# Mish's products in quarters and normalising products in halves, shared between VectorE and GpSimd

## The chip, the cores and the metric

The kernel runs on one core of one Trainium2 chip. The metric is the device time of one execution in microseconds (us), from a few runs of the same program; lower is better.

## What is computed

The reference mixes two branches over the same input x (2048 tokens of 640 values) with one gate per token:

```python
x = A_x
g = _sigmoid((x * gate_w).sum(-1, keepdims=True))
a = _A_ref(x, A_wqkv, A_wo)     # softmax attention, 32 heads of 20, then @ wo
b = _B_ref(x, B_w1, B_b1, B_w2) # h = x@w1 + b1;  h * tanh(softplus(h));  @ w2
return g * a + (1 - g) * b
```

The activation h·tanh(log(1+exp h)) is Mish, over 2048 x 1536 values. Attention has 32 heads x 2048 x 2048 scores, and every one of them goes through an exponential.

## The kernel before

**Units and slots.** The scores are cut into 2048 units of 128 keys x 512 queries. A *group* (c, g) is one chunk c of 512 queries with four heads g; it has 64 units. The program goes through them in 683 slots of three units (`NSLOT`). For each slot TensorE writes three blocks of 512 columns into PSUM (`score_mms`, L1330), and ScalarE takes the exponential of them in one ACTIVATE (`emit_e`, L1351). TensorE multiplies the results with V into one PSUM bank for the group (`pv`, L1669).

**Units given to VectorE.** In many slots the third unit is not given to ScalarE. VectorE evicts it from PSUM as a 16-bit integer that serves as a rough exponential (`emit_x`, L1400). Two more VectorE passes from SBUF to SBUF, over up to four such units at a time, make two shifted copies (`shift`, L1438), and TensorE multiplies all three with V. ScalarE then has an ACTIVATE of 1024 columns in that slot instead of 1536. `choose` (L1497) decides for each slot whether a unit is given away: it adds up how far VectorE is behind and what is waiting for it, and refuses from `BEHIND`, from `crowded` (`IDLE`, `IDLE_2`: how much may wait when the slots before gave one too), when tasks are late (`CATCH_UP`, `LAG`), or when `room` finds that the rest would not fit. `NUDGE` is a list of 87 hand-set values, one for every eight slots, which shifts that sum.

**Other work.** Everything else is put in between: projections of q, k and v, the Mish branch (`h_task`: x@w1 and a bias add on VectorE, L1040; then `mish`; then `b_task`: @w2), and the output products (`p_task`, `part_task`). One Mish covers 128 x 1024 values and there are 24 of them. Each is a tanh on ScalarE (L1063) and then a chain of eight VectorE steps, each of which reads what the one before wrote: a 16-bit copy W, three short tensor-scalar steps (both L1087), and four products of two 16-bit tensors (L1090). W and the second tensor B exist once, so one Mish is in work at a time. The steps wait in the queue `blend`, which is worked off from its head.

**Normalising.** When a group is finished, its sums are copied out of PSUM (L1849). Its 128 x 16 denominators go by DMA to another layout, are inverted on GpSimd with a power instruction (`invert`, L1871), and go by DMA through DRAM to all rows (L1874, L1880). Then one product of 128 x 512 normalises the group (`times`, L1805). For the last groups of the last chunk (`DIRECT`) VectorE makes the inverse by itself with two transposes (L1860 to L1862). The partial output products of the last chunk (`part_task`) are placed by `PART_DUE`.

**What sets the order.** The whole order is worked out in Python when the program is built. `Plan` keeps a clock for each engine; `Plan.add` appends an instruction, advances the clock by a cost constant (`WIDE` 0.60 us for a wide VectorE pass, `EXP` 1.335 and `EXP_PAIR` 0.908 for the two kinds of ACTIVATE, `INVERT`, `ASIDE` for GpSimd) and records semaphore waits. The times of the plan are not the chip's: on the chip only the order on each engine and the waits hold. `work` fills VectorE with waiting jobs before an eviction is due. After each eviction `settle` (L498) looks back at VectorE's line in the plan: instructions from SBUF to SBUF carry the mark "L". If the head of `blend` or `norm` may go to GpSimd, if it is ready, and if its GpSimd cost and 0.1 us fit between the last such instruction and VectorE's clock, it is put on GpSimd, with a wait for that last instruction. Before, this holds for the normalising product alone, as a whole. `patient` keeps a job from VectorE until a short time after it is ready. `load` counts a job that may go to GpSimd with 0.3 (`SHARE`) of its cost.

Of the kernel before, what the change touches and what calls it, by code (L numbers as in the profile page):

```python
# [14 lines left out]
ALU = mybir.AluOpType  # L15
# [14 lines left out]
CW = 512  # L30
# [4 lines left out]
SCALE = DH ** -0.5  # L35
EW = DH + 1
NETS = 6
OLD = 3
WAITED = 2
OWE = 0.1  # L40
SLOT = 3
HALF = D // 2

# [20 lines left out]
FLEX = 1  # L64
TOP_UP = 0
SX = 285
SX_STEP = 15
AWAIT = 0.01
SHARE = 0.3
AWAIT_1 = 0  # L70
# [4 lines left out]
LANES = 2  # L75
TAKEN = 3.6
LATE_OFF = 0.4
SLACK = 0.2
LATER = 0.5
FREE = 0  # L80
# [9 lines left out]
NEAR = 0.2  # L90
STORED = 1.0
TALL = 0.1
BEYOND = 0.4
SOONER = 9
KT_AHEAD = 5
NEXT_KT = 2
QUAD = 0.60
# [13 lines left out]
EAGER = 90  # L111
LOAD = 0.95
MISH = 4
GROUP = 3.0
LAST = 0
END = 55
SHIFT = 0.5
LAG = 50
SPARE = 3
WINDOW = 4.0  # L120
CALM = 2
PACKED = 5
PACKED_Q = 21
Q_AT = 120
Q_STEP = 21
SQ = 40
SQ_STEP = 16
H_AT = 150
H_STEP = 14
# [25 lines left out]
WARM = 7  # L155
FETCH = (2.3, 3.0)
LEAD = 16
NUDGE = [0.8, -6, -3.5, -3.7, 3.7, 3, -3.7, 3, -3, 1.5, 1.5, 5.3, 3.7, 3, -0.7, -1.5, 6, 0.0, 6, 0.7, -0.7, -5.2, 0.7, -0.7, 0, 3.7, -3, 1.5, 0.7, -4.3, 2.2, 5.3, 3.7, 1.5, 1, 2.2, -0.8, 2.1, 2.9, 2.3, 1.5, 6, 5.0, 5.9, -3, -2.3, -2.3, 1.5, 1.5, 1.5, 1.5, 2.0, 1.5, -5, -3.5, 0.8, 5, 0.0, 0.7, 2.9, 0.7, 1.5, 0, 6, 6, 5, 3.6, 6, 6, 5.8, 6, -0.8, 3.8, 1.5, 2.2, 5.7, 0.7, 5, 6, 2.2, 6, 4.5, 3.0, -1.5, 5, 0.5, 5]


class Op:
# [113 lines left out]
def bass_gated_mix__softmax_full_mha__dense_activation_mish__prompt_kernel(  # L275
# [44 lines left out]
    RR = sb("RR", [P, 16], FP32)  # L320
# [36 lines left out]
    BC = BCT[:, :]  # L357
# [72 lines left out]
    def attention(pl, fast):  # L430
# [3 lines left out]
        at = {}  # L434
# [63 lines left out]
        def settle():  # L498

            while fast:  # L500
                for todo in (blend, norm):
                    job = todo[0][5] if todo and len(todo[0]) > 5 else None
                    ready = job and job[0]()
                    if not ready:
                        continue
                    line = pl.line
                    i = len(line)
                    while i and not line[i - 1][2]:
                        i -= 1
                    begin = max(ready.t1 + HOP, pl.now["pool"], line[i - 1][0])  # L510
                    while i < len(line) and line[i][0] <= begin:
                        i += 1
                    if begin + job[1] + APART <= pl.now["dve"]:
                        todo.popleft()
                        job[2](line[i - 1][1])
                        break
                else:
                    return

        def patient(op, wait):  # L520

            return now["step"] < NSLOT - CALM_END and pl.now["dve"] < op.t1 + wait
# [86 lines left out]
        if fast:  # L609
# [448 lines left out]
            def mish(ev, hb, hc, k):  # L1058


                h = hb.rearrange("p i t -> p (i t)")
                U = AREAS[6 * hc + k >= FIRST][2]
                ex = pl.add("act", lambda e: e.activation(U, h, AF.Tanh, scale=0.5, bias=-MISH_AT), [ev, u_free[0]], cost=0.95)  # L1063
                u_free[0] = "busy"
                last = [ex]
                due = ex.t1 + PATIENCE

                def piece(cost, fn, after=None, wait=0):
                    def run(eng="dve", *more):
# [12 lines left out]

                W, B = (U2[:, n * CW:(n + 1) * CW].bitcast(FP16) for n in range(2))

                def scalar(dst, src, one, two=None):
                    ops = (one, two, ALU.mult, ALU.add) if two is not None else (one, None, ALU.add)
                    return lambda e: e.tensor_scalar(dst, src, *ops)  # L1087

                def times(dst, one, two):
                    return lambda e: e.tensor_tensor(dst, one, two, ALU.mult)  # L1090
# [5 lines left out]
                piece(WIDE, times(B, B, B))  # L1096
                piece(QUICK, scalar(B, B, MISH_BY, MISH_BY * MISH_OUT), None, AWAIT_1)
                piece(WIDE, times(B, W, B))
                piece(WIDE, times(h, B, h), done)

            def b_task(hc, t, half, due):
                c, part = divmod(hc, 2)
# [663 lines left out]
        def group_done(c, g, step, last):  # L1766
# [36 lines left out]
            def times(src, deps, eng="dve"):  # L1803
                to = otn(c, g, fast) if direct else OTN[:, moves[0] % 2, NFT, :]
                op = oung_free[0] = bc_read[0] = otn_done[(c, g)] = pl.add(eng, lambda e: e.tensor_tensor(  # L1805
                    to, src, BC, ALU.mult), [*deps, *reads()], cost=WIDE if eng == "dve" else ASIDE, kind="L")
# [63 lines left out]
            def invert():  # L1870
# [1 line left out]
                    RR[:, :], RR[:, :], NEG[:, :].to_broadcast([P, 16]), ALU.pow), [got, m_neg], cost=INVERT)  # L1872
                     if fast else pl.add("dve", lambda e: e.reciprocal(RR[:, :], RR[:, :]), [got], cost=0.25))
                rr_read[0] = pl.add("sp", lambda e: e.dma_start(  # L1874
                    SUMS.ap().rearrange("j (r a) -> (j r) a", a=16), RR[:, :]), [r, *spread_last], "nr1", cost=0.4, tail=2.8)
                norm.append((0.0, spread, lambda: rr_read[0]))

            def spread():
                for j in range(HG):
# [4 lines left out]
                norm.append((WIDE, lambda: times(src, wide), lambda: False if fast and patient(wide[-1], AWAIT) else wide[-1],  # L1884
                             0, None, (lambda: wide[-1], ASIDE, lambda dep: times(src, [*wide, dep], "pool"))))
            norm.append((0.25, invert, lambda: got))


# [461 lines left out]
```

## Time and profile before

| | |
|---|---|
| median of 3 runs | 761.59 us (760.7 to 762.83) |
| profiled execution: its own time | 759.97 us |
| its span, first to last instruction | 758.2 us |
| granted TensorE clock | 0.997 |
| instructions | 19479 |

The busy times of the engines in the span overlap; a share near 100% means that the engine hardly pauses. An instruction's duration in the trace reaches into the next one's start, so that on a queue without pauses the distance from start to start is what an instruction costs. "Idle before" is time in which the engine waited ahead of an instruction, with what ended the wait behind the arrow. VectorE is DVE in the profile, ScalarE ACT, TensorE PE, GpSimd POOL.

### The profile page before, as it was taken

Reading aid. Unit: us, or ns where it says so; the run is one execution under the profiler, and the core shown is the slowest. Engines: PE = TensorE matmul, PEld = TensorE weight load, DVE = VectorE, ACT = ScalarE, POOL = GpSimd, SP = SyncE. Lnnn points to the kernel's source line nnn. Section 1 sums busy time; section 2 is a strip of 40 time slices with the busy share of each in tenths; the row PEclk is TensorE's granted clock in tenths of the full one; section 3 lists DMA queues with packets and bytes.
Section 4 is the critical chain, followed back from the end, with each engine's and each line's share of the span. In section 5 each row is a group of like instructions: output and inputs, shape, how many; then the busy total and the mean of one; then the engine's idle time right before and its main releaser. Section 6 shows DMA issues by size and latency. Waiting matters only on the chain.

```text
span 758.2 us, 19479 instructions
## 1 busy us (share of the span) xinstructions
PE 717.1 (95%) x8095; PEld 266.2 (35%) x8095; DVE 705.2 (93%) x1275; ACT 742.7 (98%) x714; POOL 124.8 (16%) x62
## 2 busy tenths in 40 slices
PE   8999999999999999999999999999999998999996
PEld 4433332333323333333333344333333333333233
DVE  4789899999999899998989999999999999999997
ACT  6999999999999999999999999999999999999996
POOL 8112120211110121110222100211022110211000
PEclk9999999999999999999999999999999999999999
DMA  8311321211233223150212414021221221010001
GB/s 186 106 56 53 99 64 51 69 54 54 65 94 114 64 65 91 37 147 20 66 43 82 111 32 124 28 70 51 68 62 48 68 67 38 19 31 21 22 8 39
DMA packets 80737, 49.05 MB, mean 65 GB/s; under 512 B 24794, under 2 KB 76882, under 8 KB 80642
## 3 DMA queue, kind: packets, MB, share of 16 engines
q1 hardware_dynamic: 79874, 47.61, 22.4%
q8 instruction: 67, 1.10, 0.6%
q14 instruction: 28, 0.23, 0.1%
q10 hardware_dynamic: 656, 0.10, 0.1%
q0 software_dynamic: 112, 0.01, 0.1%
HBM read 35.57 MB, written 7.51 MB: 57 GB/s over the span
## 4 chain that ended last, share of the span: by engine, by line
ACT 77%; PE 11%; DVE 10%; DMA 1%; issue 0%; SPq 0%
ACT ETS L1351 75%; PE PS L1330 3%; PE PS L1669 3%; PE PS L567 2%; DVE OTN L1400 2%; ACT REG L1063 2%; DVE OTN L1438 1%; PE PS L2077 1%; DVE U L1087 1%; DVE U L1090 1%; DVE REG L1400 1%; DVE HB L1040 1%; ACT W2R L1063 1%; DMA OTN<-in_A_x_dram 1%; DVE QT L1400 1%; DVE PADS L1400 1%
## 5 line engine op out<-in xcount | busy, mean ns | idle before, releaser
L1351 ACT ACTIVATE ETS<-PS 128x1024 bf16<-128x1024 f32 (+1 forms) x683 | 722.4, 1264 | 3.9 <-PE PS L1330 3.3
L1330 PE MATMUL PS<-QT,KT 32*128 32x512 bf16 (+1 forms) x2112 | 270.2, 378 | 22.5 <-ACT ETS L1351 16.4
L1871 POOL TENSOR_TENSOR RR<-RR,NEG 128x16 f32<-128x16 f32 x29 | 90.1, 3106 | 470.4 <-DMA RR<-OUNG 413.8
L1669 PE MATMUL PS<-ETS,V_all 128*21 128x512 bf16 (+1 forms) x1621 | 161.1, 376 | 0.0
L1330 PEld LDWEIGHTS PS<-QT,KT 32*128 32x128 bf16 x2112 | 67.3, 91 | 230.9 <-ACT ETS L1351 182.3
L567 PE MATMUL PS<-XB,REG 128*32 128x256 bf16 (+3 forms) x770 | 82.4, 295 | 4.3 <-DVE HB L1040 2.2
L1400 DVE TENSOR_SCALAR QT<-PS 128x512 int16<-128x512 f32 x116 | 78.4, 684 | 4.8 <-PE PS L1330 3.9
L567 PE MATMUL PS<-W2R,HB 128*32 128x320 bf16 (+1 forms) x747 | 70.3, 300 | 3.3 <-DVE XB L1112 1.5
L1400 DVE TENSOR_SCALAR OTN<-PS 128x512 int16<-128x512 f32 x105 | 70.7, 683 | 1.5 <-PE PS L1330 1.2
L1400 DVE TENSOR_SCALAR PADS<-PS 128x512 int16<-128x512 f32 x85 | 57.1, 682 | 5.5 <-PE PS L1330 5.1
L567 PEld LDWEIGHTS PS<-XB,REG 128*128 128x128 bf16 (+1 forms) x770 | 38.4, 96 | 38.5 <-issue 27.3
L1669 PEld LDWEIGHTS PS<-ETS,V_all 128*21 128x21 bf16 x1621 | 39.2, 90 | 34.4 <-issue 29.8
L1090 DVE TENSOR_TENSOR U<-U 128x1024 f16<-128x1024 f16 x72 | 49.1, 682 | 0.2
L567 PEld LDWEIGHTS PS<-W2R,HB 128*32 128x32 bf16 (+1 forms) x747 | 33.6, 97 | 33.7 <-issue 13.7
L1400 DVE TENSOR_SCALAR REG<-PS 128x512 int16<-128x512 f32 x60 | 40.6, 683 | 2.5 <-PE PS L1330 2.0
L1400 DVE TENSOR_SCALAR KT<-PS 128x512 int16<-128x512 f32 x49 | 33.4, 685 | 3.8 <-PE PS L1330 3.5
L1040 DVE TENSOR_TENSOR HB<-PS,B1T 128x512 bf16<-128x512 f32 x48 | 32.7, 682 | 2.2 <-PE PS L567 2.0
L1805 POOL TENSOR_TENSOR OTN<-OUNG,BCT 128x512 bf16<-128x512 f32 x12 | 15.2, 1270 | 94.8 <-issue 76.7
L1087 DVE TENSOR_SCALAR U<-U 128x1024 f16<-128x1024 f16 x72 | 30.1, 418 | 0.6
L567 PE MATMUL PS<-XB,WOQ 128*128 128x512 bf16 (+1 forms) x146 | 28.6, 382 | 0.7 <-DVE HB L1040 0.5
L1438 DVE TENSOR_SCALAR QT<-QT 128x2048 int16<-128x2048 int16 (+2 forms) x48 | 28.7, 603 | 0.4 <-PE PS L1669 0.4
L1400 DVE TENSOR_SCALAR W2R<-PS 128x512 int16<-128x512 f32 x38 | 25.7, 684 | 2.2 <-PE PS L1330 1.5
(174 smaller groups left out, 778.6 us busy)
## 6 DMA issues: line engine op xcount, KB each, us to landing
REG<-in_B_w_dram SPq DMA_DIRECT2D x36, 320.0 KB, 3.2
BCT<-SUMS SPq DMA_DIRECT2D x116, 64.0 KB, 2.1
W2R<-in_B_w_dram SPq DMA_DIRECT2D x12, 320.0 KB, 3.3
KT<-KS SPq DMA_DIRECT2D x28, 128.0 KB
QT<-QS SPq DMA_DIRECT2D x112, 20.0 KB
QS<-WOQ SPq DMA_DIRECT2D x16, 128.0 KB, 1.8
KS<-OTN SPq DMA_DIRECT2D x16, 128.0 KB, 1.8
W2R<-in_B_w_dram SPq DMA_DIRECT2D x1, 1920.0 KB, 8.4
```

What stands on the lines that cost most here:

```text
L567: op = e.matmul(PS[at, bank, cols], w[:, at], x, start=start, stop=stop, **({"tile_position": (0, i * rows)} if parts > 1 else {}))
L1040: ev = dve(lambda e: e.tensor_tensor(hb, PS[:, bank, :].rearrange("p (i t) -> p i t", i=2), bias, ALU.add), [last, b_load, *b_read.get(hc ...
L1063: ex = pl.add("act", lambda e: e.activation(U, h, AF.Tanh, scale=0.5, bias=-MISH_AT), [ev, u_free[0]], cost=0.95)
L1087: return lambda e: e.tensor_scalar(dst, src, *ops)
L1090: return lambda e: e.tensor_tensor(dst, one, two, ALU.mult)
L1330: op = pl.add("pe", lambda e, i=i, g=real(g), tile=tile, j=j, cols=cols, c=c, of_q=of_q: e.matmul(scores(s)[:, i, cols], KT[32 * j:32 * j ...
L1351: e_op[s] = pl.add("act", lambda e: e.activation(EXPS[:, at:at + n, :], scores(s)[:, 0:n, :], AF.Exp, scale=SCALE, bias=LIFT if fast else ...
L1400: ev = dve_by(lambda e: e.tensor_scalar(block(batch["y"], n, I16), scores(s)[:, 2, :], SCALE * ULPS, BIAS, ALU.mult, ALU.add), [s_op[s], * ...
L1438: op = pl.add("dve", lambda e, sp=sp: e.tensor_scalar(some_of(home, sp, I16), some_of(y, sp, I16), by, None, ALU.add), deps, cost=each, ki ...
L1669: lasts[n] = pl.add("pe", lambda e, v=v, j=j, src=src[:, cols], of_q=of_q, count=count: e.matmul(PS[32 * j:32 * j + EW, bank, of_q], v, sr ...
L1805: op = oung_free[0] = bc_read[0] = otn_done[(c, g)] = pl.add(eng, lambda e: e.tensor_tensor(to, src, BC, ALU.mult), [*deps, *reads()], cos ...
L1871: r = (pl.add("pool", lambda e: e.tensor_tensor(RR[:, :], RR[:, :], NEG[:, :].to_broadcast([P, 16]), ALU.pow), [got, m_neg], cost=INVERT) ...
```

## The change

Each of Mish's four products may now be taken by GpSimd in quarters of 256 columns, as long as they fit beside VectorE's evictions; VectorE takes what is left of the product in one instruction. It waits until 0.2 us after the product is ready (`AWAIT_2`). The normalising product is treated in the same way in two halves. `DIRECT` goes from 3 to 1, so that groups (3, 5) and (3, 6) are normalised by way of GpSimd and DMA as the others are. The plan's cost of the power instruction goes from 0.6 to 2.9 us, and the store behind it counts 0.7 us instead of 2.8. Many constants of the plan are changed with it, and `NUDGE`. The list of `NUDGE` is not one that was set for products in four pieces.

```diff
-OLD = 3
+OLD = 4
-OWE = 0.1
+OWE = 0.3
-STREAM = 0.34
-SPUN = 0.4
+STREAM = 0.3
+SPUN = 0.45
-INVERT = 0.6
+INVERT = 2.9
+ASIDE_2 = 0.7
+PARTS = 2
+MPARTS = 4
+ASIDE_M = 0.75
+AWAIT_2 = 0.2
+TAKE_M = 1
-SLACK = 0.2
+SLACK = 0.3
-FILL = 2.5
-GIVE_BACK = 50
+FILL = 2.0
+GIVE_BACK = 60
-IDLE_2 = 6
+IDLE_2 = 11
-SOONER = 9
+SOONER = 10
-BEHIND = 9.0
+BEHIND = 11.0
-CATCH_UP = 10
+CATCH_UP = 8
-LOAD = 0.95
-MISH = 4
-GROUP = 3.0
+LOAD = 1.05
+MISH = 3.25
+GROUP = 4
-LAG = 50
-SPARE = 3
-WINDOW = 4.0
-CALM = 2
+LAG = 40
+SPARE = 5
+WINDOW = 5.2
+CALM = 3
-DIRECT = 3
+DIRECT = 1
-PART_DUE = 18
-LAST_DUE = 21
+PART_DUE = 57
+LAST_DUE = 23
...
@@ settle
-                        todo.popleft()
-                        job[2](line[i - 1][1])
+                        if job[2](line[i - 1][1]) is not False:
+                            todo.popleft()
@@ mish
-                piece(WIDE, times(B, W, B))
+                def product(dst, one, two, after=None):
+                    made, size = [], 2 * CW // MPARTS
+
+                    def part(n, m):
+                        at = slice(n * size, m * size)
+                        return lambda e: e.tensor_tensor(dst[:, at], one[:, at], two[:, at], ALU.mult)
+
+                    def end(op):
+                        last[0] = op
+                        if after:
+                            after(op)
+
+                    def beside(dep):
+                        n = len(made)
+                        made.append(pl.add("pool", part(n, n + 1), [last[0], dep, *made], cost=ASIDE_M, kind="L"))
+                        entry[0] = WIDE * (MPARTS - n - 1) / MPARTS + 0.06
+                        if n + 1 == MPARTS:
+                            end(made[-1])
+                        return n + 1 == MPARTS
+
+                    def rest():
+                        end(pl.add("dve", part(len(made), MPARTS), [last[0], *made], cost=entry[0], kind="L"))
+
+                    dep = lambda: False if patient(last[0], AWAIT_2) else made[-1] if made else last[0]
+                    entry = [WIDE, rest, dep, due, None, (lambda: last[0] if TAKE_M else None, ASIDE_M, beside)]
+                    blend.append(entry)
+
+                product(B, W, B)
...
@@ spread (normalising)
+                def beside(dep):
+                    n = len(made)
+                    made.append(times(src, [*wide, dep, *made], "pool", cols_of(n), n + 1 == PARTS))
+                    entry[0] = WIDE * (PARTS - n - 1) / PARTS + 0.04
+                    return n + 1 == PARTS
+
+                def rest():
+                    times(src, [*wide, *made], "dve", slice(len(made) * CW // PARTS, CW))
```

More of the change, by code (lines that the diff above doesn't have):

```diff
@@ L66 @@
 SX = 285
-SX_STEP = 15
+SX_STEP = 17
 AWAIT = 0.01
@@ L1087, in scalar @@
                     return lambda e: e.tensor_scalar(dst, src, *ops)
[L1089 to L1090 removed]
                 piece(WIDE, scalar(W, U, 1.0), read)
                 piece(QUICK, scalar(B, W, MISH_IN), None, AWAIT_1)
[L1094 removed]
+                def product(dst, one, two, after=None):
[20 more added lines that the diff above has]
+                product(B, W, B)
                 piece(QUICK, scalar(B, B, MISH_MID), None, AWAIT_1)
[L1096 removed]
+                product(B, B, B)
                 piece(QUICK, scalar(B, B, MISH_BY, MISH_BY * MISH_OUT), None, AWAIT_1)
[L1098 to L1099 removed]
+                product(B, W, B)
+                product(h, B, h, done)
             def b_task(hc, t, half, due):
@@ L1801, in move, with times @@
                 return ops
-            def times(src, deps, eng="dve"):
+            def times(src, deps, eng="dve", cols=slice(0, CW), last=True):
                 to = otn(c, g, fast) if direct else OTN[:, moves[0] % 2, NFT, :]
-                op = oung_free[0] = bc_read[0] = otn_done[(c, g)] = pl.add(eng, lambda e: e.tensor_tensor(
-                    to, src, BC, ALU.mult), [*deps, *reads()], cost=WIDE if eng == "dve" else ASIDE, kind="L")
+                share = (cols.stop - cols.start) / CW
+                op = pl.add(eng, lambda e: e.tensor_tensor(
+                    to[:, cols], src[:, cols], BC[:, cols], ALU.mult), [*deps, *reads()],
+                    cost=WIDE * share + 0.04 * (share < 1) if eng == "dve" else ASIDE if share == 1 else ASIDE_2, kind="L")
+                if not last:
+                    return op
+                oung_free[0] = bc_read[0] = otn_done[(c, g)] = op
                 if not direct:
```

31 lines of the change are left out of this document (19 added, 12 removed).

## The prediction

> **What bounds the kernel now.** I read the page's busy times and its chain of waits first.
>
> ```profile
> PE 717.1 (95%) x8095; PEld 266.2 (35%) x8095; DVE 705.2 (93%) x1275; ACT 742.7 (98%) x714; POOL 124.8 (16%) x62
> ...
> ACT 77%; PE 11%; DVE 10%; DMA 1%; issue 0%; SPq 0%
> ```
>
> ScalarE (ACT) is busy 98% of the span and carries 77% of the chain. VectorE (DVE) stands at 93%, GpSimd (POOL) at 16%. A share over the whole span hides stages, so next the table by stretches: before Mish, the first Mishes, a stretch where they come thickest, the rest of them, the end. Columns are the length, then busy time and instructions of PE, PEld, DVE, ACT and POOL.
>
> ```profile
> 20.00:140.00 120.00, 118.05 (x1317) 42.37 (x1310) 105.10 (x190) 120.00 (x117) 20.54 (x11) 1.00 0.23 67
> 140.00:395.00 255.00, 245.37 (x2588) 86.05 (x2587) 240.43 (x433) 253.89 (x249) 39.19 (x15) 1.00 0.25 71
> 395.00:490.00 95.00, 88.67 (x1083) 37.85 (x1085) 92.25 (x170) 95.00 (x86) 13.32 (x5) 1.00 0.27 77
> 490.00:675.00 185.00, 174.79 (x2022) 65.49 (x2019) 181.27 (x327) 184.77 (x179) 31.79 (x13) 1.00 0.19 52
> 675.00:750.00 75.00, 70.08 (x890) 24.70 (x887) 72.20 (x129) 74.06 (x73) 3.08 (x2) 0.98 0.07 19
> ```
>
> From 20 to 750 us ScalarE pauses for 2.3 us in all. So the time is what lies on ScalarE, with some 28 us at the two ends. What lies there is decided by how many units are given to VectorE, and VectorE is as full: from 140 on it pauses for 23.9 of 610 us, and from 395 on for 9.3 of 355. The two trade against each other. The price of that trade stands in ScalarE's groups, kept apart by shape:
>
> ```profile
> L1351 ACT ACTIVATE ETS<-PS 128x1024 bf16<-128x1024 f32 x477 | 480.9, 1137 | 2.2 <-PE PS L1330 1.8
> L1351 ACT ACTIVATE ETS<-PS 128x1536 bf16<-128x1536 f32 x206 | 316.2, 1558 | 1.7 <-PE PS L1330 1.5
> ```
>
> A unit given away makes an ACTIVATE 1558 - 1137 = 421 ns shorter: 0.42 us. 477 of 683 slots do that now.
>
> **The change, part by part.** The rows of what it touches, kept apart by shape:
>
> ```profile
> L1090 DVE TENSOR_TENSOR U<-U 128x1024 f16<-128x1024 f16 x72 | 49.1, 682 | 0.2
> L1438 DVE TENSOR_SCALAR QT<-QT 128x2048 int16<-128x2048 int16 x35 | 23.9, 683 | 0.4 <-PE PS L1669 0.4
> L1090 DVE TENSOR_TENSOR HB<-U,HB 128x1024 bf16<-128x1024 f16 x24 | 16.4, 681 | 0.1
> L1805 DVE TENSOR_TENSOR OTN<-OUNG,BCT 128x512 bf16<-128x512 f32 x18 | 12.3, 681 | 0.0
> L1438 DVE TENSOR_SCALAR QT<-QT 128x1024 int16<-128x1024 int16 x10 | 4.2, 416 | 0.0
> L1862 DVE STREAM_TRANSPOSE BCT<-RR 128x512 f32<-128x512 f32 x2 | 1.4, 702 | 0.0
> L1860 DVE STREAM_TRANSPOSE BCT<-OUNG 128x512 f32<-128x512 f32 x2 | 1.4, 702 | 0.0
> L1861 DVE RECIPROCAL RR<-BCT 128x16 f32<-128x16 f32 x2 | 0.5, 255 | 0.1
> ```
>
> ```profile
> L1871 POOL TENSOR_TENSOR RR<-RR,NEG 128x16 f32<-128x16 f32 x29 | 90.1, 3106 | 470.4 <-DMA RR<-OUNG 413.8 <-DVE U L1087 44.8 <-DVE OUTT L1153 11.9
> L1805 POOL TENSOR_TENSOR OTN<-OUNG,BCT 128x512 bf16<-128x512 f32 x12 | 15.2, 1270 | 94.8 <-issue 76.7 <-DMA BCT<-SUMS 11.4 <-DVE W2R L1438 6.7
> ```
>
> How a product lies on GpSimd now is seen in the timelines of VectorE and of GpSimd around 415 us:
>
> ```profile
> 414.52 0.68 DVE L1438 TENSOR_SCALAR OTN<-QT 128x2048 int16<-128x2048 int16 x1
> 415.13 0.68 DVE L1040 TENSOR_TENSOR HB<-PS,B1T 128x512 bf16<-128x512 f32 x1
> 415.73 1.28 DVE L1400 TENSOR_SCALAR QT<-PS 128x512 int16<-128x512 f32 x2
> 416.93 0.68 DVE L1090 TENSOR_TENSOR U<-U 128x1024 f16<-128x1024 f16 x1
> ```
>
> ```profile
> 415.34 1.27 POOL L1805 TENSOR_TENSOR OTN<-OUNG,BCT 128x512 bf16<-128x512 f32 x1 [10.74 <-issue]
> ```
>
> It starts when the SBUF pass of 414.52 is over, lies beside three reads of PSUM, and ends at 416.61, before the next SBUF pass at 416.93. The plan's picture holds on the chip. On VectorE a wide pass costs 0.60 us from start to start (414.52, 415.13, 415.73), not its duration of 0.68.
>
> *Mish's products.* 72 + 24 = 96 of them at 0.60 us are 57.6 us of VectorE. How many quarters GpSimd will find room for no row shows. The bounds are none and all. The nearest row is the normalising product: 12 of 31 went to GpSimd (39%; 18 and one more stayed), each needing 1.27 us of room. A quarter has 256 columns, half of that row's 512, and so takes between 0.64 us (were all of 1.27 by the column, and its types as fast) and 1.27 (were it all fixed cost): it needs less room; but four in a row are wanted, and VectorE waits only 0.2 us for them. I take 30%: 17.3 us of relief. An instruction that takes only the rest of a product still pays its fixed part: 2 x 416 - 683 = 149 ns by the two shift rows, of which 80 ns lie over the neighbour, so 0.07 us; at half the products, 48 x 0.07 = 3.4 us. Net relief 13.9 us, with 0 and 57.6 as its ends.
>
> The Trainium skill ("GPSIMD Engine Reference", section 3.1) gives about 2.6 cycles an element for a two-input product on GpSimd; by its clock of 1.2 GHz I estimate 1.11 us for 512 columns and 0.55 for a quarter, without dispatch. The row of 1.27 us agrees with 0.16 us on top, which makes a quarter 0.71, inside my bounds; the sum does not change.
>
> *Normalising in halves.* 19 products on VectorE, 11.4 us. Half the room is needed for each half; I take 60% of 31 instead of 39%, which is 6.5 products x 0.60 = 3.9, less the fixed parts about 3.5 us. Ends: 0 and 11.4.
>
> *DIRECT.* Two groups lose two transposes and a reciprocal: 2 x (0.702 + 0.255 + 0.702), less 0.08 of overlap each, 2.8 us off VectorE. They gain a power instruction of 3.1 us on GpSimd and the DMA path, which is longer. The timelines of VectorE (first two and last) and of GpSimd show both:
>
> ```profile
> 476.74 0.68 DVE L1849 COPY OUNG<-PS 128x512 f32<-128x512 f32 x1
> ...
> 732.10 0.68 DVE L1849 COPY OUNG<-PS 128x512 f32<-128x512 f32 x1
> ...
> 737.20 0.68 DVE L1805 TENSOR_TENSOR QT<-OUNG,BCT 128x512 bf16<-128x512 f32 x1
> ```
>
> ```profile
> 491.07 1.27 POOL L1805 TENSOR_TENSOR OTN<-OUNG,BCT 128x512 bf16<-128x512 f32 x1 [8.75 <-issue]
> ```
>
> By DMA it is 14.3 us from copy to product (476.74 to 491.07), on VectorE 5.1. The later of the two groups would be normalised at about 746 instead of 737. What hides the 9 us is the last group, whose exponentials run to about 750. Nothing but the closing output products waits for it; without that cover it costs up to 9 us. I cost it at nothing.
>
> *Waits that are added.* A piece on GpSimd waits for a VectorE pass, and behind it on GpSimd's queue stands the next power instruction; behind that, on SP's queue, the store of the sums, then the loads and output stores.
>
> ```profile
> SPq L1874 <- POOL RR L1871: 72.7, 27, 5.9
> ```
>
> SP's queue already waits 72.7 us in 27 places there. A few quarters ahead of the power instruction delay a group's normalising by 1 to 3 us; groups follow each other by over 20 us, so I take nothing. On VectorE the rest of a product now waits for the last quarter, with evictions queued behind it; the plan puts it where it thinks the quarter done. *Plan costs.* The power instruction counted as 2.9 instead of 0.6 changes no instruction; it keeps products from being planned behind one that is still running.
>
> *The constants.* BEHIND 11, IDLE_2 11, SPARE 5 and LOAD 1.05 let more units be given away; CATCH_UP 8, LAG 40 and GROUP 4 fewer. The stretches bound the gain: VectorE's pauses from 20 to 750 are 38.8 us. The loss has no row; I take nothing, and leave it to the rivals.
>
> *Sum.* Relief 13.9 + 3.5 + 2.8 = 20.2 us. A unit given away costs VectorE 0.60 for the eviction and two shifts of 0.60 for four units, 0.30: 0.90 us, and every unit also shortens the span by 0.42. So 20.2 / (0.90 + 0.42) = 15.3 units, and 15.3 x 0.42 = 6.4 us. TensorE gets two more passes for each unit, some 0.1 us each: 3 us on an engine with 31 us of pauses between 140 and 750. The profiled execution of 759.97 us (span 758.2, 1.8 around it) becomes 753.6. The median of the runs is 1.6 above that execution, so I forecast 755.2.
>
> **The rivals.** *More is taken.* GpSimd takes half of Mish (28.8 us, less fixed parts 26) and the looser limits fill half of VectorE's pauses (19): with 6.3 for the rest 51 us, 39 units, 16 us, so about 745. For it: GpSimd is idle 84% of the span. Against: quarters are wanted only while a Mish is in work, between 140 and 675.
>
> *The pieces hold VectorE up.* If a VectorE pass that needs SBUF stood still while a quarter runs, each meeting would cost up to 0.64 us (half of 1.27). Some 115 quarters, half of them met, half a length each: 57 x 0.32 = 18 us, which eats the relief of 20.2: 761, no change. If all were met in full it is 74 us lost, 53 net, 17 us slower. The trace speaks against it, in VectorE's timeline and GpSimd's:
>
> ```profile
> 577.16 0.68 DVE L1090 TENSOR_TENSOR U<-U 128x1024 f16<-128x1024 f16 x1
> 577.76 0.68 DVE L1438 TENSOR_SCALAR OTN<-OTN 128x2048 int16<-128x2048 int16 x1
> ```
>
> ```profile
> 576.82 4.38 POOL L1871 TENSOR_TENSOR RR<-RR,NEG 128x16 f32<-128x16 f32 x1 [11.86 <-DVE OUTT L1153]
> ```
>
> The power instruction ran beside SBUF passes and took 4.38 instead of 3.11; the two shown stayed at 0.68. GpSimd gave way. The Trainium skill ("SBUF — State Buffer", "Who interferes with whom") has it that a VectorE instruction with two SBUF inputs or in a two-port mode and a GpSimd instruction exclude each other for a whole instruction, and that whichever starts first goes first. By that rule a quarter that runs late stops VectorE, which is this rival; the rows show only the other order.
>
> *VectorE is given more than it can carry* (the slower side). A job that may go to GpSimd is counted by the plan with 0.3 of its cost. If GpSimd takes 30% of Mish, VectorE keeps 70%, and 57.6 x 0.4 = 23 us of its work is not counted when units are given away, with looser limits beside. Then evictions come late, the scores two slots on wait for them, and ScalarE pauses. Were 15 units too many given away, VectorE would be 15 x 0.90 = 13.5 us over, and the time 755.2 + 13.5 = 768.7. The thick stretch is where it would start; evictions there, by stretches:
>
> ```profile
> 140.00:395.00 255.00, 120.38 (x179) 1.00 0.25 71
> 395.00:490.00 95.00, 24.64 (x37) 1.00 0.27 77
> ```
>
> 37 in 95 us against 179 in 255: there Mish already crowds units out. For it: VectorE has 2.75 us left in that stretch. Against: the plan's clock of VectorE does count what it keeps, and `choose` refuses once it is behind. It decides from the point where ScalarE's pauses grow by more than 6.4 us.
>
> *Nothing is taken.* If quarters rarely fit, only the normalising and DIRECT remain: 6.3 us of relief, 2 us: 759.6, no change that a measurement tells.
>
> **How the numbers follow.** A measurement of this kernel tells about 0.3% (2.3 us) from no change. Forecast 0.48, more is taken 0.13, pieces hold VectorE up 0.08 (mostly no change), nothing taken 0.08, VectorE overloaded 0.23. Faster: 0.48 + 0.13, less a little for the forecast's weak end, 0.60. Same 0.16, slower 0.24. The forecast's own range is 751 to 758 (GpSimd's share 50% to 15%: 32 to 12 us of relief, 10.3 to 3.9 us). To leave out no more than 2 in 10 the range goes from 747, into the first rival, to 767, into the overload.
>
> **What would show it.** Right: about 492 ACTIVATEs of 1024 columns instead of 477; some 115 GpSimd products of 256 columns at 0.6 to 0.8 us; the L1090 rows of VectorE down from 65 to about 50 us; ScalarE's pauses still about 2 us from 20 to 750. Overload: more than 492, and ScalarE waiting on scores behind late evictions. Held up: VectorE passes longer than 0.70. Nothing taken: hardly any quarters. I am wrong if the count of short ACTIVATEs falls although quarters are taken: then the order, not the relief, decides.

## The result and the profile after

The changed kernel takes 767.32 us (median of 4 runs, 765.64 to 772.84) where the kernel before took 761.14 beside it (4 runs, 759.1 to 762.83): a ratio of 1.0104 with a 95% interval of 1.008 to 1.0129. It is slower by 1.0%. The profiled execution took 765.64 us with a span of 763.8, against 759.97 and 758.2: 5.7 us more, and I take that difference apart.

The page of the kernel after, first the busy times, then the chain of work that ended last:

```profile
PE 716.5 (94%) x8135; PEld 267.8 (35%) x8135; DVE 700.7 (92%) x1288; ACT 743.0 (97%) x718; POOL 181.3 (24%) x156
...
ACT 73%; PE 20%; DVE 3%; DMA 2%; POOL 1%; issue 1%; SPq 0%; POOLq 0%
```

GpSimd took on work (124.8 to 181.3 us) and VectorE lost some, as the change wants. ScalarE is as busy as before, in a longer span. The same five stretches show whether it pauses more:

```profile
20.00:140.00 120.00, 116.50 (x1284) 41.49 (x1272) 105.14 (x190) 119.55 (x116) 19.20 (x11) 1.00 0.23 68
140.00:395.00 255.00, 243.93 (x2577) 86.34 (x2571) 240.19 (x435) 253.13 (x248) 52.52 (x41) 1.00 0.24 70
395.00:490.00 95.00, 89.07 (x1070) 35.94 (x1064) 91.06 (x172) 94.94 (x90) 25.75 (x26) 1.00 0.27 76
490.00:675.00 185.00, 173.45 (x2036) 65.51 (x2034) 179.28 (x332) 184.10 (x177) 50.40 (x49) 0.99 0.19 54
675.00:750.00 75.00, 71.47 (x918) 26.99 (x918) 70.58 (x134) 74.84 (x72) 13.28 (x9) 1.00 0.09 25
```

It hardly does: 0.45 + 1.87 + 0.06 + 0.90 + 0.16 = 3.4 us, against 2.3. Nor does it have more to do. Its groups, kept apart by shape:

```profile
L1381 ACT ACTIVATE ETS<-PS 128x1024 bf16<-128x1024 f32 x484 | 483.5, 1106 | 3.6 <-PE PS L1360 2.5
L1381 ACT ACTIVATE ETS<-PS 128x1536 bf16<-128x1536 f32 x199 | 301.2, 1530 | 1.5 <-PE PS L1360 1.2
```

484 short ACTIVATEs instead of 477: seven more units given away, 7 x 0.42 = 2.9 us less on ScalarE. So nothing between 20 and 750 us explains a loss, and the next place to look is what comes after the last exponential. ScalarE's timeline from 744 us on, of the kernel after:

```profile
744.67 6.48 ACT L1381 ACTIVATE ETS<-PS 128x1536 bf16<-128x1536 f32 x5
754.60 0.95 ACT L1248 ACTIVATE PADS<-PS,GATE 128x320 f32<-128x320 f32 x2 [3.45 <-PE PS L573]
756.16 0.53 ACT L1248 ACTIVATE PADS<-PS,GATE 128x320 f32<-128x320 f32 x1 [0.62 <-POOL HB L1251]
757.80 0.53 ACT L1248 ACTIVATE PADS<-PS,GATE 128x320 f32<-128x320 f32 x1 [1.10 <-POOL HB L1251]
```

And the same place before, where this line is ScalarE's last:

```profile
743.61 7.86 ACT L1351 ACTIVATE ETS<-PS 128x1536 bf16<-128x1536 f32 x6
```

The last exponential ends at 744.67 + 6.48 = 751.15, before at 743.61 + 7.86 = 751.47: 0.3 us earlier. From there to the end of the span it is 12.65 us instead of 6.7: **6.0 us more after the last exponential, which is the whole difference**. What fills them is four closing output products of the last chunk (`p_task` with `rest`) that had to be done after the last slot; there the kernel closes them by an ACTIVATE each (L1248) and an addition on GpSimd (L1251), one waiting for the other. VectorE's and GpSimd's timelines of the kernel after:

```profile
697.67 0.68 DVE L1102 TENSOR_TENSOR HB<-U,HB 128x1024 bf16<-128x1024 f16 x1
...
727.44 0.68 DVE L1836 TENSOR_TENSOR OTN<-OUNG,BCT 128x512 bf16<-128x512 f32 x1
...
730.04 0.55 DVE L1142 TENSOR_SCALAR XB<-PS,OMG 128x320 bf16<-128x320 f32 x1 [0.71 <-PE PS L573]
...
753.41 0.54 DVE L1183 SCALAR_TENSOR_TENSOR W2R<-PS,GATE,XB 128x320 f32<-128x320 f32 x1
```

```profile
755.20 2.50 POOL L1251 TENSOR_TENSOR HB<-PADS,W2R 128x320 bf16<-128x320 f32 x3 [9.80 <-ACT PADS L1248]
758.40 0.86 POOL L1251 TENSOR_TENSOR HB<-PADS,W2R 128x320 bf16<-128x320 f32 x1 [0.70 <-ACT PADS L1248]
```

VectorE's timeline before, at the corresponding places:

```profile
674.12 0.68 DVE L1090 TENSOR_TENSOR HB<-U,HB 128x1024 bf16<-128x1024 f16 x1
...
703.86 0.54 DVE L1112 TENSOR_SCALAR XB<-PS,OMG 128x320 bf16<-128x320 f32 x1
...
715.86 0.68 DVE L1805 TENSOR_TENSOR OTN<-OUNG,BCT 128x512 bf16<-128x512 f32 x1
...
741.79 0.54 DVE L1153 SCALAR_TENSOR_TENSOR W2R<-PS,GATE,XB 128x320 f32<-128x320 f32 x1
...
746.51 0.55 DVE L1153 SCALAR_TENSOR_TENSOR HB<-PS,GATE,W2R 128x320 bf16<-128x320 f32 x1 [0.39 <-PE PS L567]
...
750.72 0.55 DVE L1153 SCALAR_TENSOR_TENSOR HB<-PS,GATE,W2R 128x320 bf16<-128x320 f32 x1 [0.54 <-PE PS L567]
```

Read the pairs. The last product of the last Mish starts at 697.67 instead of 674.12; the last `b_task` (the XB rows) at 730.04 instead of 703.86; the last partial output product (the last W2R row) at 753.41 instead of 741.79. These three hang together in the code: `part_task` is not ready before every `b_task` is done (`len(bdone) < 2 * NTB`, L1271), and a closing product not before its partial one. The same line asks for groups (3, 0) to (3, 5) to be normalised, and the row of 727.44 is group (3, 5), 11.6 us later than at 715.86. So both conditions of the partial products moved; after, the `b_task` came last of the two, by 2.5 us (730.59 against 728.12). Before, the four closing products then ran on VectorE from 746.51 to 751.27 while exponentials still went on. After, the last partial product alone ends 2.8 us behind the last exponential, and the closing products come behind it.

### The profile page after: what moved, and what is told of

Read it like the earlier page. It is cut to its first block, busy times and chain, and to the rows that moved or that the text cites. A ratio compares the mean times of both kernels' runs of the same rounds, so it can differ in the third digit from the quotient of the medians.

```text
span 763.8 us, 19737 instructions
## 1 busy us (share of the span) xinstructions
PE 716.5 (94%) x8135; PEld 267.8 (35%) x8135; DVE 700.7 (92%) x1288; ACT 743.0 (97%) x718; POOL 181.3 (24%) x156
## 4 chain that ended last, share of the span: by engine, by line
ACT 73%; PE 20%; DVE 3%; DMA 2%; POOL 1%; issue 1%; SPq 0%; POOLq 0%
ACT ETS L1381 70%; PE PS L1360 7%; PE PS L1699 6%; PE PS L573 4%; ACT REG L1069 2%; PE PS L2130 2%; PE PS L912 1%; ACT W2R L1069 1%; DMA OTN<-in_A_x_dram 1%; DMA RR<-OUNG 1%; PE PS L783 1%; POOL HB L1251 0%; POOL RR L1906 0%; DMA SUMS<-RR 0%; DMA BCT<-SUMS 0%
## 5 line engine op out<-in xcount | busy, mean ns | idle before, releaser
L1102 POOL TENSOR_TENSOR U<-U 128x256 f16<-128x256 f16 x69 | 45.0, 652 | 212.6 <-DVE U L1093 167.3
L1430 DVE TENSOR_SCALAR QT<-PS 128x512 int16<-128x512 f32 x123 | 83.3, 685 | 6.5 <-PE PS L1360 5.4
L1430 DVE TENSOR_SCALAR PADS<-PS 128x512 int16<-128x512 f32 x89 | 60.3, 685 | 5.4 <-PE PS L1360 5.0
L573 PEld LDWEIGHTS PS<-XB,REG 128*32 128x32 bf16 (+1 forms) x821 | 40.7, 98 | 33.9 <-issue 22.0
L1430 DVE TENSOR_SCALAR REG<-PS 128x512 int16<-128x512 f32 x64 | 43.5, 685 | 0.9 <-PE PS L1360 0.5
L1102 DVE TENSOR_TENSOR U<-U 128x768 f16<-128x768 f16 (+3 forms) x72 | 39.9, 554 | 0.0
L1430 DVE TENSOR_SCALAR KT<-PS 128x512 int16<-128x512 f32 x43 | 29.1, 686 | 3.8 <-PE PS L1360 3.6
L573 PE MATMUL PS<-XB,WOQ 128*32 128x512 bf16 (+1 forms) x167 | 29.0, 382 | 0.5 <-DVE QT L703 0.2
L1836 POOL TENSOR_TENSOR OTN<-OUNG,BCT 128x256 bf16<-128x256 f32 x13 | 9.5, 728 | 78.3 <-issue 58.3
L1468 DVE TENSOR_SCALAR QT<-QT 128x2048 int16<-128x2048 int16 (+2 forms) x46 | 25.8, 572 | 0.2
```

What stands on the lines that cost most here:

```text
L573: op = e.matmul(PS[at, bank, cols], w[:, at], x, start=start, stop=stop, **({"tile_position": (0, i * rows)} if parts > 1 else {}))
L1102: return lambda e: e.tensor_tensor(dst[:, at], one[:, at], two[:, at], ALU.mult)
L1430: ev = dve_by(lambda e: e.tensor_scalar(block(batch["y"], n, I16), scores(s)[:, 2, :], SCALE * ULPS, BIAS, ALU.mult, ALU.add), [s_op[s], * ...
L1468: op = pl.add("dve", lambda e, sp=sp: e.tensor_scalar(some_of(home, sp, I16), some_of(y, sp, I16), by, None, ALU.add), deps, cost=each, ki ...
```

## Experiments

Three theories. **O**: the order does not fit the pieces; `NUDGE` and the constants lead to a plan in which Mish ends late, and the quarters themselves help. **P**: the quarters themselves cost the time, because a chain of Mish in which VectorE and GpSimd wait for each other takes longer (on average 13.3 us from first to last step, 11.6 before). **D**: the way of groups (3, 5) and (3, 6) over GpSimd and DMA makes the end late. The experiments carry the names e1 to e10. They were run beside the kernel before, whose medians were 761.0 (e1 to e4), 761.11 (e5 to e8) and 760.96 us (e9, e10).

**e1, no quarters** (on the kernel after):

```diff
-TAKE_M = 1
+TAKE_M = 0
```

> The changed kernel with TAKE_M = 0: Mish's products stay whole on VectorE, all else as changed, the order worked out anew by the same constants. Theory O (the order): the loss comes from a greedy order whose constants and NUDGE do not fit it; the pieces themselves relieve VectorE by some 11 us and are worth 3 to 6 us. Then this is slower than the changed kernel, 769 to 775 us. Theory P (the pieces): quarters lengthen Mish's chains (11.6 to 13.3 us on average), so the last Mish is done at 698 instead of 675 us and the last tasks come after the last exponential. Then this is back at 759 to 763 us, with the last Mish at about 675.

Measured: 775.64 us, ratio 1.0188 (1.0159 to 1.0218), so 8.3 us slower than with the quarters. ScalarE's groups and the end of its timeline:

```profile
L1381 ACT ACTIVATE ETS<-PS 128x1024 bf16<-128x1024 f32 x475 | 475.4, 1112 | 8.7 <-PE PS L1360 7.8
```

```profile
744.63 16.05 ACT L1381 ACTIVATE ETS<-PS 128x1024 bf16<-128x1024 f32 x14
764.16 0.95 ACT L1248 ACTIVATE PADS<-PS,GATE 128x320 f32<-128x320 f32 x2 [3.49 <-PE PS L573]
```

The last exponential ends 9.5 us later (760.7), with nine fewer units given away and more waits. The four late closing products are there without any quarter, and a Mish takes 13.7 us on average. That speaks against P. But taking the quarters out moves the order too, so it does not yet say what a quarter is worth. (The outputs of e1 and e2 are off from the reference by a relative error of 0.028 and 0.023; why was not traced, and only their times are used here.)

**e2, groups (3, 5) and (3, 6) on VectorE again** (on the kernel after):

```diff
-DIRECT = 1
+DIRECT = 3
```

> The changed kernel with DIRECT = 3 again, so that groups (3, 5) and (3, 6) are normalised on VectorE. Theory D (the direct path): the DMA path normalises (3, 5) at 727 instead of 716 us, the partial products wait for it, and this makes the 5.9 us longer end. Then 761 to 763 us here. Theories O and P: the partial products were late because the tasks ahead of them were; 766 to 769 us, within 2 us of the changed kernel.

Measured: 770.62 us, 1.0131 (1.0095 to 1.0167). Its closing ACTIVATEs:

```profile
744.14 12.08 ACT L1381 ACTIVATE ETS<-PS 128x1536 bf16<-128x1536 f32 x9
760.48 0.99 ACT L1248 ACTIVATE PADS<-PS,GATE 128x320 f32<-128x320 f32 x2 [4.26 <-PE PS L573]
```

With the short way back, the end after the last exponential is 13.4 us long, not shorter than 12.65. Group (3, 5) is normalised by 724.1 here, 32 us ahead of the last exponential instead of 23, and the end is no shorter: a late Mish (it ends at 702.6, the last `b_task` at 734.4) is enough for it. For group (3, 6) this run says little, since its sums were ready 13 us later (743.83 instead of 730.92); e9 below settles that. I had expected this run within 2 us of the changed kernel, and it is 3.3 us slower.

**e3, how much one value of the order is worth** (on the kernel before, the 16th of the 87 values):

```diff
 NUDGE = [
...
-3, -0.7, -1.5, 6,
+3, -0.7, -0.8, 6,
...
```

> The kernel before with one of the 87 values of NUDGE changed, the 16th (slots 120 to 127) from -1.5 to -0.8; nothing else. Theory O: the order behind it falls anew, and an order that was not set for it costs about as much as the change cost or more, 5 to 25 us, with Mish and the closing tasks later, as in the changed kernel. Theories P and D: a shift of 0.7 us in one sum does nothing that is measurable, 760 to 763 us.

Measured: 783.22 us, 1.0277 (1.0238 to 1.0317). Not a line of the work changed, three more units were even given away, and it costs 22 us:

```profile
L1351 ACT ACTIVATE ETS<-PS 128x1024 bf16<-128x1024 f32 x480 | 478.5, 1107 | 16.1 <-PE PS L1669 7.9 <-PE PS L1330 7.2
```

ScalarE pauses 18.0 us instead of 2.3, Mish ends at 702.5, four closing products are left over. One of the pauses is 6.84 us long. ScalarE's timeline behind it, and TensorE's within it:

```profile
636.13 1.94 ACT L1351 ACTIVATE ETS<-PS 128x1024 bf16<-128x1024 f32 x2 [6.84 <-PE PS L1669]
```

```profile
631.25 0.40 PE L1669 MATMUL PS<-PADS,V_all 128*21 128x512 f16 x4 [0.74 <-DVE PADS L1438]
631.85 0.40 PE L1669 MATMUL PS<-QT,VW 128*21 128x512 f16 x4 [0.21 <-DVE QT L1438]
633.66 0.61 PE L1669 MATMUL PS<-PADS,VW 128*21 128x512 f16 x4 [1.41 <-DVE PADS L1438]
635.07 0.61 PE L1669 MATMUL PS<-OTN,V_all 128*21 128x512 f16 x4 [0.80 <-DVE OUNG L1849]
```

A group had to be closed, its last units had been given to VectorE, and TensorE stood still for the shifted copies (L1438); the scores for ScalarE were queued behind.

**e4, the functions of the change with all the old constants** (on the kernel after; the 32 values that differ, `NUDGE` among them, set as before; nine of them, `STORED` and `EAGER` for example, are missing from the list in the section on the change):

```diff
-OLD = 4
+OLD = 3
...
-BEHIND = 11.0
+BEHIND = 9.0
...
-DIRECT = 1
+DIRECT = 3
-PART_DUE = 57
+PART_DUE = 18
...
```

> The changed functions (quarters, halves) with all the plan's constants and NUDGE as they were before. Theory O: quarters relieve VectorE, but the old order does not fit either: 764 to 770 us. Theory that the new constants are at fault and the pieces good: 755 to 759 us. Theory P: as the changed kernel or slower for the pieces alone, last Mish late, 766 us or more.

Measured: 783.17 us, 1.0275 (1.0221 to 1.0329); 489 short ACTIVATEs, 22.0 us of pauses, 94 quarters on GpSimd, last Mish 715.4. I had expected 764 to 770. A list that gave 761 us for whole products gives 783 for products in pieces. Together with e3 this shows how little such a list carries over.

**e5, the same order without the overlap** (on the kernel after): the plan is made as it is, and then the 85 quarters are issued on VectorE at their places in the plan. (VectorE's rows below hold four more quarters, which were its own already.)

```diff
+    back_again = []
...
                         made.append(pl.add("pool", part(n, n + 1), [last[0], dep, *made], cost=ASIDE_M, kind="L"))
+                        back_again.append(made[-1])
...
+    for op in back_again:
+        op.eng = op.key = "dve"
```

> The changed kernel with its order kept exactly; only the 85 quarters that GpSimd takes are issued on VectorE instead, at the place in its queue at which they were planned. VectorE gets 85 instructions of about 0.2 us more (0.133 for the columns, 0.07 fixed), 17 us, two thirds of it in stretches where it pauses for under 3%. Theory O: the quarters on GpSimd are worth something in any one order: slower than the changed kernel by 5 to 17 us, 772 to 784 us. Theory P (quarters on GpSimd cost more than they relieve): faster than the changed kernel or equal, 762 to 767 us.

Measured: 775.44 us, 1.019 (1.0151 to 1.0228). VectorE's quarters and ScalarE's groups:

```profile
L1103 DVE TENSOR_TENSOR U<-U 128x256 f16<-128x256 f16 x73 | 20.4, 279 | 0.0
...
L1103 DVE TENSOR_TENSOR HB<-U,HB 128x256 bf16<-128x256 f16 x16 | 4.5, 280 | 0.0
```

```profile
L1383 ACT ACTIVATE ETS<-PS 128x1024 bf16<-128x1024 f32 x484 | 478.7, 1079 | 5.8 <-PE PS L1362 3.5
```

The same 484 units are given away, but VectorE now has the quarters too, and the time is 8.1 us longer than with them on GpSimd: 8.6 us of ScalarE's pauses instead of 3.4, the last exponential at 760.7, Mish at 707.9. With the order held, the quarters on GpSimd are worth about 8 us. P falls: they shorten this order.

**e6, one other value of the list** (on the kernel after, the 25th value):

```diff
 NUDGE = [
...
-1.5, 3.7, 0, 3,
+2.2, 3.7, 0, 3,
...
```

> The changed kernel with the 25th value of NUDGE (slots 192 to 199) at 2.2 instead of 1.5, nothing else. Theory O: another order falls out, with as good a chance to be better as worse since this list was not set for the quarters; the last Mish is done earlier, at some 680 us, and no closing task is left for after the last exponential: 758 to 762 us. Theories P and D: quarters, chains and the path of (3, 6) are as they were, 766 to 768 us.

Measured: 763.46 us, 1.0024 (1.0009 to 1.004): 3.9 us better from one value, though not the 758 to 762 that I expected. No closing product is left over and the end after the last exponential is 7.5 us; but ScalarE pauses 9.3 us with 489 short ACTIVATEs, and its last exponential ends at 755.6.

**e7, the list set anew for the pieces** (on the kernel after). Single steps are tried, 1,500 in all, and a step is kept when the plan's own clock ends no later; 61 of 87 values changed. Nothing else is.

```diff
 NUDGE = [
-2.3, -4.5, -3.5, -3.7, 3.7,
+4.5, -5.3, -3.5, -6, 3.7,
...
```

> The changed kernel with NUDGE set anew by a blind search of single steps (1,500 tries, 61 of 87 values moved), nothing else. Theory O: faster than the kernel before, 752 to 758 us; 488 short ACTIVATEs, pauses of ScalarE as before, end no longer than before. Theory P: quarters cost, whatever the order: 762 us or more.

Measured: 759.32 us, 0.9973 (0.9957 to 0.9988), 8.0 us less than the changed kernel; I had expected 752 to 758.

```profile
L1381 ACT ACTIVATE ETS<-PS 128x1024 bf16<-128x1024 f32 x489 | 489.0, 1123 | 1.5 <-PE PS L1360 0.9
```

489 short ACTIVATEs and 2.4 us of pauses: the last exponential ends at 747.2, 4.3 us earlier than before. Three closing products are still left over (Mish ends at 693.2), and the end after it is 9.5 us.

**e8, no quarters, the list set anew with the same search** (on the kernel after):

```diff
-TAKE_M = 1
+TAKE_M = 0
...
 NUDGE = [
-2.3, -4.5, -3.5, -3.7, 3.7,
+3.0, -4.5, -3.5, -6, 3.7,
...
```

> As the run before it, but with Mish's products whole on VectorE (TAKE_M = 0), and NUDGE set anew by the same search with as many tries. What the quarters are worth between two orders that were each set for themselves. Theory O: 2 to 6 us slower than with quarters, 756 to 762 us, with 6 or more short ACTIVATEs fewer. Theory P: faster than with quarters.

Measured: 760.7 us, 1.0 (0.9984 to 1.0016), with 483 short ACTIVATEs. The search alone brings 14.9 us here (from 775.64), and 1.4 us are left between quarters and no quarters, with intervals that overlap a little; I had expected 2 to 6.

**A longer search, with the quarters** (e9, 66 of 87 values changed) **and without them** (e10, 64):

```diff
 NUDGE = [
-2.3, -4.5, -3.5, -3.7, 3.7,
+2.1, -6, -3.5, -4.5, 3.7,
...
```

> The changed kernel with NUDGE set anew by a longer search (two starts, 5,500 tries each, the better one; 66 of 87 values moved), nothing else. Theory O: faster than the kernel before and than the search with 1,500 tries (759.3): 754 to 757 us, 489 short ACTIVATEs, last exponential some 6 us before that of the kernel before, no closing task after it. Theory P: no better than 759.

```diff
-TAKE_M = 1
+TAKE_M = 0
...
 NUDGE = [
-2.3, -4.5, -3.5, -3.7, 3.7,
+-1.6, -6, -3.5, -5.2, 3.7,
...
```

> The same longer search with Mish's products whole on VectorE (TAKE_M = 0; one start). Theory O: 3 to 6 us slower than with quarters, 758 to 761 us, about 481 short ACTIVATEs. Theory P: as fast as with quarters or faster.

Measured: 758.75 us, 0.9971 (0.9949 to 0.9992), with quarters; 759.91, 0.9985 (0.9965 to 1.0004), without. The two searches are not quite alike: e9 is the better of two starts, e10 has one. Both ends after the last exponential are 6.7 us, with no closing product left over: 751.47 before, 750.19 and 751.3 here for the last exponential. For e9 I had expected 754 to 757, and for e10 3 to 6 us more than e9; both missed. ScalarE's row and the end of its timeline:

```profile
L1381 ACT ACTIVATE ETS<-PS 128x1024 bf16<-128x1024 f32 x490 | 487.9, 1111 | 4.4 <-PE PS L1360 3.6
```

```profile
743.65 6.54 ACT L1381 ACTIVATE ETS<-PS 128x1536 bf16<-128x1536 f32 x5
```

The 13 units more than before are there (13 x 0.42 = 5.5 us), yet the last exponential is only 1.3 us earlier. ScalarE's pauses from 20 to 750 are 4.2 us instead of 2.3. The rest shows in the starts. Where nothing holds it up, an exponential costs 0.904 us (short) or 1.331 us (long) from its start to the next; what all exponentials take beyond that sums to 13.7 us before, 16.3 after and 17.5 in e9. So of the 5.5 us, 3.9 went into later starts, only half of them pauses that the busy times show (an ACTIVATE's duration reaches into the next one's start, and the mean of the short form fell from 1137 to 1111 ns), and 0.4 into a later first exponential. What held those starts up was not traced one by one.

The end after the last exponential follows the number of closing products left over, through all of these kernels: 6.7, 6.7 and 6.7 us with none (before, e9, e10) and 7.5 in e6; 8.6 with two (e8); 9.5 with three (e7); 12.65 to 14.4 with four (after, e1 to e5). That number in turn follows how far ahead of the last exponential the last partial product ends: 9.1 us before, 3.9 in e9 and e10 and 2.8 in e6 leave none; 1.3 in e8 leaves two; 0.9 in e7 leaves three; after and in e1 to e5 it ends behind the last exponential, and four are left.

D falls as the cause of the loss: e9 keeps the way over GpSimd and DMA, normalises (3, 6) at 744.3, as late as the changed kernel (743.8), and leaves nothing over. But that way uses up margin. In e8 to e10 Mish ends by 685, and the first partial product follows the normalising of (3, 5) by 5.4 to 5.8 us, much as before (5.3); (3, 5) is done at 723.6 to 727.5 there instead of 716.5, and in e8, the latest of them, two closing products are left over. How the 6.0 us divide between a late Mish and a late (3, 5) was not measured.

O holds: the functions and the constants of the change are the same in after, e6, e7 and e9, and `NUDGE` alone moves the time from 767.3 to 758.8. That the quarters help is shown for one fixed order (e5); between two orders set anew it is hardly shown.

## Why the prediction was wrong

**Bound, and the price of a unit: right.** ScalarE paused 3.4 us from 20 to 750, and a unit given away is worth 1530 - 1106 = 424 ns.

**Mish's products: right in kind, a little smaller.** The rows of the kernel after: GpSimd's by shape, Mish's first three products on VectorE from the page (all shapes in one row), and VectorE's normalising by shape:

```profile
L1102 POOL TENSOR_TENSOR U<-U 128x256 f16<-128x256 f16 x69 | 45.0, 652 | 212.6 <-DVE U L1093 167.3 <-DVE REG L1468 15.6 <-DVE QT L1468 10.3
...
L1102 POOL TENSOR_TENSOR HB<-U,HB 128x256 bf16<-128x256 f16 x16 | 10.9, 683 | 29.0 <-DVE U L1102 16.6 <-DVE OTN L1468 5.0 <-DVE QT L1468 3.1
L1836 POOL TENSOR_TENSOR OTN<-OUNG,BCT 128x256 bf16<-128x256 f32 x13 | 9.5, 728 | 78.3 <-issue 58.3 <-DVE V_all L893 13.4 <-DVE OUTT L964 6.4
...
L1836 POOL TENSOR_TENSOR QT<-OUNG,BCT 128x256 bf16<-128x256 f32 x2 | 1.5, 728 | 7.4 <-DVE U L1865 7.3
```

```profile
L1102 DVE TENSOR_TENSOR U<-U 128x768 f16<-128x768 f16 (+3 forms) x72 | 39.9, 554 | 0.0
```

```profile
L1836 DVE TENSOR_TENSOR OTN<-OUNG,BCT 128x512 bf16<-128x512 f32 x18 | 12.3, 683 | 1.8 <-DMA BCT<-SUMS 1.8
L1836 DVE TENSOR_TENSOR OTN<-OUNG,BCT 128x256 bf16<-128x256 f32 x11 | 4.5, 411 | 0.0
```

85 quarters of 384, 22% where I took 30; each 0.65 to 0.68 us on average, at the lower of my bounds. They lie in 56 of the 96 products (by shape, VectorE has 40 products whole and 31, 21 and 4 with one, two and three quarters gone), and VectorE took the rest of every one of them. VectorE's products of Mish went from 65.5 to 54.2 us (the 39.9 above, and 14.3 for the last products): 11.3 us of relief where the sum had 13.9.

**Normalising in halves: wrong sign.** 15 halves went to GpSimd, 7.5 of 31 products (24%) instead of 12 (39%): VectorE's normalising rose from 13.0 to 12.3 + 4.5 = 16.8 us. I had 3.5 us of relief; it is a loss of 3.8. The step that failed is "Half the room is needed for each half; I take 60%". By the rows, 13 products found room, where 12 did before; but of 11 of them GpSimd got one half and VectorE took the other (its 11 rows of 256 columns), and only two went over whole. So the smaller piece hardly raised the number of products that found room, and halved what most of them gave. That the quarters took the room is not it, since without quarters e1 has only 14 halves. Nor is it the new cost of the power instruction, since e4, which counts 0.6 as before, has 12. That VectorE takes the second half because the plan makes it wait no more than 0.01 us (`AWAIT`) is argued from the code.

**DIRECT: relief right, cost not the one I looked at.** The power instructions are 31 instead of 29 and the wide transposes are gone. Group (3, 6) was normalised at 743.8, where I had it at about 746 and before had 737. e9 shows that this did not set the end. I had not looked at group (3, 5), which the partial products wait for: from copy to product it took 13.4 us (714.02 to 727.44) instead of 6.9 (708.97 to 715.86).

**The sum: right in units, not in time.** 11.3 - 3.8 + 2.8 = 10.3 us of relief, by 1.32 us are 7.8 units; seven came, worth 2.9 us. The last exponential came only 0.3 us earlier, since by their starts the exponentials took 2.6 us more beyond their cost (16.3 against 13.7), 1.1 us of it in pauses. The sum had no term for that. So the 12.0 us between the 753.6 forecast for the profiled execution and its 765.64 divide, to 0.1, into three: 6.0 for the longer end, 3.5 for 8.3 units fewer than the 15.3, and 2.6 for those later starts.

**The failed step: the cover of the end.** "Nothing but the closing output products waits for it", I wrote of the later normalising of (3, 6); the last group's exponentials hide it, and I costed it at nothing. I checked one of the things that the closing products wait for. The other is the partial products, which wait for all of Mish through `b_task`, and for group (3, 5); they came 11.6 us later, and cost 6.0 us. The root is my sentence on the constants: "The loss has no row; I take nothing". A bound was to be had from rows of before: the last `b_task` ended at 704.4 and the first partial product started at 721.87, which is 17.5 us of margin, and the last partial product ended 9.1 us ahead of the last exponential. The last `b_task` came 26 us later (its distance behind the last Mish stayed at about 30 us), which is more than that margin covers. The place of the loss is shown (after against e9). That the order makes Mish late is shown too, by e6, e7 and e9, which change nothing but `NUDGE` and end Mish at 683.1, 693.2 and 676.6 instead of 698.4. Which decision of the plan does it was not traced.

**The rivals.** The overloaded VectorE gave 768.7, near the 767.3 measured, but its mechanism is not what happened: it needed ScalarE's pauses to grow by more than 6.4 us, and they grew by 1.1. In e4 they grew by 19.7, but not from an overloaded VectorE either: from 140 to 395 us, where 17.3 of its 22.0 us lie, VectorE is busy for 224.1 us against 240.4 before and waits itself, among others 5.8 us for the DMA of normalising products and 5.1 for GpSimd's quarters. Pieces that hold VectorE up were seen, but rarely (below). "Nothing is taken" and "more is taken" did not come. My sign for being wrong, fewer short ACTIVATEs despite quarters, did not come either: the order decided with seven more of them.

## What to carry to other kernels

Where a greedy plan with hand-set values makes the order, a change comes out as its own gain plus the luck of the new order, and here the second was up to 22 us against some 1 to 8 of the first: compare with the order held fixed (e5), or with it set anew on both sides (e7 against e8, e9 against e10). The two answer different questions: the quarters are worth 8 us in a fixed order that counts on them, and 1.2 to 1.4 us, which these runs hardly tell from nothing, between two orders each set for its own kernel. And when work is taken off the bound engine, list all that must still be done after its last instruction, follow each item back to what makes it ready, and give each its own margin.

## What the runs showed of the hardware

**VectorE and GpSimd stop each other, in either order.** The prediction's rows showed only GpSimd giving way. There the power instruction of 576.82 seems to be first, but a copy of VectorE, which those rows leave out, had begun 0.08 us before it:

```profile
576.74 0.50 DVE L1640 TENSOR_SCALAR VW<-V_all 128x1344 bf16<-128x1344 bf16 x1
```

In the kernel after, the same scaling copy of VectorE (L1670 there) met quarters; two of these meetings are shown, in VectorE's and GpSimd's timelines:

```profile
242.72 0.50 DVE L1670 TENSOR_SCALAR VW<-V_all 128x1344 bf16<-128x1344 bf16 x1
...
571.00 0.82 DVE L1670 TENSOR_SCALAR VW<-V_all 128x1344 bf16<-128x1344 bf16 x1
```

```profile
242.88 1.68 POOL L1102 TENSOR_TENSOR HB<-U,HB 128x256 bf16<-128x256 f16 x2 [2.58 <-DVE OTN L1836]
...
569.96 1.49 POOL L1102 TENSOR_TENSOR U<-U 128x256 f16<-128x256 f16 x2 [8.61 <-DVE U L1093]
```

At 242.72 the copy was first: it took its usual 0.50, and of the two quarters the first, which began 0.16 us into it, took 0.87 us instead of 0.67. At 571.00 the second quarter was under way, until 571.45, and the copy took 0.82. The Trainium skill ("SBUF — State Buffer", "Who interferes with whom") says that whichever of the two starts first holds the shared ports for its whole instruction, and this agrees. Such meetings are few: by their durations quarters and this copy held each other up three times in the whole trace (the third at 644.70, where the copy took 0.79), for 0.8 us in all. The plan places the quarters beside PSUM evictions; it does not count this copy among the passes to keep clear of.

**A lull of TensorE is paid twice.** In e3, the stretch in which TensorE waited for the shifted copies, by windows of 5 us (after the length come busy time and instructions of PE, PEld, DVE, ACT and POOL, then the granted clock):

```profile
625.00:630.00 5.00, 4.59 (x38) 1.79 (x37) 4.83 (x10) 4.29 (x5) 0.00 (x0) 1.00 0.07 16
630.00:635.00 5.00, 1.91 (x17) 0.50 (x15) 4.11 (x8) 0.00 (x0) 0.00 (x0) 0.77 0.00 0
635.00:640.00 5.00, 4.13 (x38) 0.89 (x41) 4.51 (x10) 3.77 (x4) 3.01 (x1) 0.50 0.25 67
640.00:645.00 5.00, 5.00 (x65) 2.12 (x62) 3.10 (x7) 2.90 (x4) 0.44 (x1) 0.70 0.17 47
```

In the 5 us in which TensorE is busy for 1.91, the granted clock begins to fall, to 0.77 on average; it is 0.50 in the next 5 and 0.70 in those behind. In TensorE's timeline of e3 above, four matmuls with V that start at 631.85 take 0.40 us, those from 633.66 on 0.61. The Trainium skill ("TensorE: Matmul & The Clock Gate", "What's actually happening") has the clock halved after a window in which TensorE was idle; here it was halved with TensorE busy for 1.3 of the 2.7 us before, and it stayed at 0.50 until about 643 although TensorE was busy without a pause from 639 on. So late shifted copies cost ScalarE first the wait of 6.84 us, and behind it come scores at half the clock; ScalarE pauses once more, for 2.04 us ahead of 643.58, and how much of that is the clock's was not separated.
